# B C of a chunk on eight places of 32 rows by 64 columns in four banks, with the order of work drawn anew

## The chip, the cores and the metric

The kernel runs on one core of one Trainium2 chip. The metric is the device time of one execution in microseconds, the median of several runs. Before the change it is 276.1 us (three runs, 275.99 to 276.71).

## What is computed

A chunked state-space layer feeds a bilinear feed-forward network. `x` is 4 batches x 8 heads x 768 positions x 32; `B` and `C` have a state of 16.

```python
L = np.exp(cum[:, :, :, None] - cum[:, :, None, :]) * causal
CB = np.einsum('bhin,bhjn->bhij', Cc, Bc)
y_intra = np.einsum('bhij,bhjd->bhid', CB * L, xc)
y_inter = np.einsum('bhin,bhnd->bhid', Cc, state) * decay_to_i[:, :, :, None]
state = decay_full[:, :, None, None] * state + np.sum(Bx, axis=2)
...
h = (x @ w1) * (x @ w2) @ w3
return (h @ w_out).astype(np.float32)
```

Here `cum` is the running sum of log `a` within a chunk, and `x` in the last lines is the first part's output, 3072 tokens of 256. The hidden width is 1024. The four weight matrices come as float64.

## The kernel before

**The scan part.** The sequence is cut into 16 chunks of 48 positions. A chunk `c` has 32 sequences (4 batches x 8 heads); two of them share the partitions, so there are 16 groups. Its steps, by name in the written order:

- `B`, `N`, `X` (lines 274 to 276) load B and C for the products (`bc`), B for the state (`bn`) and x (`xe`); `K` loads the running sums.
- `D0`, `D1` (line 300) compute the exponents on TensorE in the first eight chunks; `F` and `G` (lines 321 to 328) do it on VectorE or POOL in the later ones. `E0`, `E1` (line 337) apply Exp into the tile `r`.
- `CB` (line 353) multiplies B with C on TensorE. The operand has 128 rows: two halves `r` of 64 rows, and in each half two groups `p` times the two sequences of a group times the state of 16, with zeros where the rows of one sequence or group meet the columns of another. A product takes 64 rows and 64 columns of the array (rows by `r`, columns by `i`), 96 columns of moving data, and there are 4 x 2 x 2 = 16 of them. The result of half `r` lies in one PSUM bank, so CB takes two banks.
- `M0`, `M1` (line 344, VectorE) multiply `r` by that result; `W0`, `W1` (line 340, POOL) put in the state's part.
- `MX` (line 366) is the product with x and the state, on places of 64 rows by 32 columns.
- `T` (line 382, VectorE) and `Z0` to `Z7` (line 386, on three engines) carry the state into the next chunk's `xe`. `hi`, `lo` (lines 404 to 408) write the output as a rounded part and a rest into `xT`.

**The network part.** A float64 weight is loaded into `st` (`D`), and made into a rounded part and a rest by `A` (ScalarE), `L` and `S` (VectorE), `H` and `P` (any of two engines; line 424 and on). `w0` to `w7` are pieces of w1 and w2, `v00` to `v17` of w3, `o0` to `o3` of w_out. `v..M` (line 491) multiplies w3 by w_out in advance; it gathers in two banks per half for the whole time of that half, and `e` reads them out. The tokens are cut into seven blocks (384, 384, 512 x 4, 256). For block `s` and piece `f`, `ls.f.m` (line 519) has 12 matmuls into two banks, `a` and `g` read them (ScalarE, VectorE), and `h` and `l` split the product. `ds.t.m` (line 563) multiplies by the combined weight, `y` reads the result out and `x` stores it.

**What sets the order.** `PLAN` (line 25) is a list of words, `name:engine` or `name@banks`; each engine executes its words in the order of that list, the loads go to SP's queue in that order (line 137), and the banks of every TensorE step are written into it. `+6@5` stands for six matmuls of zeros that fill TensorE at the start. `st` has four buffers, `mag` five, `fr` four places for the `v` weights, `bc` two.

Of the kernel before, what the change touches and what calls it, by code (L numbers as in the profile page):

```python
# [25 lines left out]
k.act:S k.zero:V k.keep:G t.D +6@5 k.D1:D a.D c0.B c0.N c0.X t.clip:V w0.D t.ln:S k.R0:S c0.Y1:G c1.B +3@7 k.L:S c1.N a.clip:V c0.Y0:G c0.D1@0 a.ln:S  # L26
c1.X w2.D a.scan:V c1.Y1:V +3@7 w1.D a.hi:V c1.Y0:V c0.D0@1 c0.E1:S a.lo:G c0.W1:G c0.CB@2,3 c0.E0:S a.save c0.W0:G c1.D0@4 k.D2:D c0.M1:V c0.M0:V
w0.L:V c0.MX@5,6 w7.D c1.E0:S w0.A:S w0.S:V w0.H:S c1.D1@7 c1.W0:G c0.T:V c0.hi:S w0.P:V c0.Z5:S c0.Z6:S c0.Z1:G c0.lo:V c1.CB@0,1 c0.Z0:S c0.Z4:G
c1.E1:S c0.Z7:V c0.Z2:V c2.B w2.A:S w2.L:V +5@7 c2.N c1.W1:G c1.M0:V c0.Z3:S c1.M1:V w2.S:V c1.MX@2,3 w1.A:S c3.N w1.L:V w6.D c1.hi:S c1.T:V j.m@4
w2.H:V k.R1:S w4.D c1.lo:V +2@7 w2.P:G j.c:S l0.0.m@5,6 w7.A:S c2.K w7.L:V w1.S:V l0.0.a:S w7.S:V c2.CB@7,0 w1.H:V w7.H:S c3.X l0.0.g:V w1.P:G  # L30
l0.2.m@1,2 w3.D w7.P:V l0.2.a:S c2.X w6.L:V w6.A:S l0.1.m@3,4 l0.2.g:V w6.S:V w4.A:S c3.B w4.L:V v11.D w6.H:V l0.1.a:S w5.D w4.S:V c2.D0@5 c2.D1@6
l0.7.m@1,2 c2.E0:S w6.P:G l0.1.g:V c2.E1:S c3.K w4.H:S l0.7.a:S c2.W1:G c4.B w3.A:S w3.L:V l0.6.m@3,5 c2.W0:G c2.M1:V c1.Z4:S o0.D c1.Z3:G c2.M0:V
c1.Z6:G l0.7.g:V c1.Z1:G l0.6.a:S c1.Z0:V c1.Z2:V c5.N c1.Z5:V c1.Z7:V c3.CB@4,6 w3.S:V w4.P:V c2.MX@0,1 w3.H:S l0.6.g:V v11.A:S l0.4.m@7,2 c5.B
c2.T:V c2.hi:S w3.P:V c2.Z0:S c2.Z4:S c2.Z2:G c2.lo:V c2.Z1:S c4.X c2.Z6:S c2.Z5:V w5.A:S w5.L:V v10.D c3.D0@3 c2.Z7:V c3.D1@5 c2.Z3:V c4.N l0.4.a:S
l0.3.m@0,1 v11.L:V c3.E0:S c4.K w5.S:V c3.E1:S c3.W0:G l0.4.g:V w5.H:S c3.W1:G c3.M0:V l0.3.a:S c3.M1:V c4.CB@7,3 w5.P:V o0.A:S a.keep c3.MX@4,5
o0.L:V v11.S:V l0.5.m@2,0 c3.hi:S c3.T:V v11.H:S o0.S:V v11.P:G c3.lo:V l0.5.a:S c3.Z5:S l0.3.g:V o0.H:S l1.7.m@6,2 l0.5.g:V c3.Z2:S c3.Z3:G c3.Z1:S
c3.Z7:V c3.Z4:G c3.Z0:S c5.X v10.A:S v10.L:V o0.P:G c6.B c3.Z6:S l1.7.a:S o1.D c4.D0@4 c4.D1@5 l1.5.m@1,0 c4.E0:S v12.D l1.7.g:V c4.E1:S c5.K c4.W0:G
v10.S:V l1.5.a:S c4.W1:G c4.M0:V v13.D v10.H:V l1.4.m@6,4 v00.D c4.M1:V v10.P:G c7.N l1.5.g:V c6.N l1.4.a:S c4.MX@1,2 l1.4.g:V c5.CB@5,7 o1.A:S o1.L:V
c9.K c4.T:V c4.hi:S l1.6.m@3,0 o1.S:V c4.Z1:S c4.Z5:S c4.Z6:G c4.lo:V c4.Z7:G v12.A:S c4.Z4:V c6.X c4.Z2:G l1.6.a:S c4.Z3:V v01.D c4.Z0:G o1.H:V c7.B
c5.D1@6 c5.D0@4 v12.L:V l1.3.m@1,2 c5.E1:S o1.P:G l1.6.g:V c6.K c5.E0:S v13.A:S l1.3.a:S v12.S:V l1.1.m@3,6 v00.A:S c5.W1:G l1.3.g:V c5.W0:G v12.H:S  # L40
c5.M1:V v03.D v00.L:V l1.1.a:S v12.P:V c6.CB@0,4 c9.F1:G c5.M0:V c8.N l1.1.g:V c8.K c5.MX@1,2 v00.S:V v10.M@7,3 c5.hi:S c9.G1:V v00.H:S c5.T:V c5.lo:V
v01.A:S c5.Z5:G c7.X c5.Z4:G l1.0.m@5,6 c5.Z6:S c5.Z1:V c5.Z3:G c5.Z2:S v00.P:V c5.Z0:S c5.Z7:S c8.B c9.F0:V l1.0.a:S v01.L:V v13.L:V c6.D1@1 c6.D0@2
v01.S:V v11.M@7,3 c6.E1:S c7.K c6.E0:S c6.W1:G l1.0.g:V v03.A:S c6.W0:G c6.M1:V l1.2.m@5,1 c9.N c6.M0:V v01.H:S v13.S:V c8.F0:G l1.2.a:S v02.D v13.H:S
v04.D v12.M@7,3 o3.D v01.P:V c8.G0:G l1.2.g:V c7.D1@2 c7.D0@6 c8.F1:V c6.MX@4,5 c7.E1:S v13.P:G c7.E0:S c7.CB@0,1 c6.T:V c8.X c6.hi:S c6.hj:S c6.lo:V
c8.E0:S c8.CB@2,6 c9.B c6.lp:V c6.Z1:G v02.A:S v02.L:V l2.7.m@4,5 c10.B c6.Z4:G c8.G1:V c7.W1:G c8.E1:S v02.S:V v04.A:S c10.K c6.Z3:G c7.M1:V l2.7.a:S
c8.W0:G v02.H:V l2.0.m@1,4 o3.A:S c7.W0:G c8.M0:V c8.W1:G c10.N c7.M0:V c11.N v02.P:V l2.0.a:S c6.Z5:V c6.Z2:V c6.Z0:V c6.Z6:V v03.L:V c8.M1:V
l2.3.m@2,0 v03.S:V c6.Z7:V v14.D o3.L:V l2.3.a:S c9.G0:V v05.D o3.S:V c10.F1:G l2.0.g:V c7.MX@1,2 o3.H:S l2.3.g:V v13.M@7,3 c7.hi:S c9.X o3.P:G c7.T:V
c9.E0:S c7.lo:V c7.Z7:S c7.Z5:S l2.7.g:V c7.Z0:S c7.Z1:G l2.2.m@6,4 v14.A:S c7.Z4:G v14.L:V c7.Z3:S c9.W0:G c7.Z2:S c9.E1:S v14.S:V l2.2.a:S c11.K
c9.W1:G v05.L:V c12.N c10.G1:G l2.5.m@0,1 l2.2.g:V c7.Z6:V c10.F0:V l2.5.a:S v04.L:V c10.G0:G c8.MX@5,6 l2.5.g:V c11.F1:G v00.M@2,4 c8.hi:S c8.T:V
c10.X c10.E0:S v04.S:V c8.Z4:S c8.Z5:G c8.lo:V c8.Z3:S o2.D c8.Z7:S c11.F0:G l2.6.m@0,1 v15.D c8.Z1:S v03.H:S v17.D c8.Z0:V c10.E1:S c10.W0:G c8.Z6:V  # L50
c12.K l2.6.a:S c10.W1:G c8.Z2:V v03.P:V c13.N v01.M@2,4 c11.G0:V v05.A:S c11.G1:V o2.A:S o2.L:V v05.S:V c9.CB@5,6 o2.S:V v06.D v02.M@2,4 c11.B c9.M0:V
v16.D o2.H:V v14.H:V o2.P:G c9.M1:V l2.4.m@0,5 l2.6.g:V v04.H:V v14.P:G l2.4.a:S v03.M@2,4 v04.P:V v15.L:V v15.A:S v06.L:V v06.A:S v05.H:V v14.M@7,3
v15.S:V v17.A:S v06.S:V v07.D v15.H:S v04.M@2,4 v17.L:V v06.H:V v17.S:V l2.1.m@6,1 v06.P:G l2.4.g:V v16.L:V l2.1.a:S v17.H:V v15.P:V v17.P:G v15.M@7,3
l2.1.g:V v07.L:V c9.MX@5,6 v05.P:V c10.CB@0,1 c12.F1:V v07.A:S c11.X c9.T:V c12.G1:G v16.A:S v05.M@2,4 c10.M0:V c12.B c9.hi:S c10.M1:V c11.E0:S
c9.Z6:G c9.Z4:G c11.E1:S c9.lo:V v16.S:V c9.Z7:S c13.K l3.0.m@0,1 c9.hj:S c11.W0:G v16.H:S c9.lp:V c11.W1:G c9.Z3:V c14.N c9.Z5:V v16.P:V l3.0.a:S
c9.Z0:V c9.Z1:V c12.F0:V v16.M@7,3 c9.Z2:V v07.S:V c12.G0:V v06.M@2,4 v07.H:V c13.F0:V v07.P:G l3.0.g:V v17.M@7,3 c13.F1:V c13.G0:V v07.M@2,4
e11.a:S@3 c13.G1:G e10.a:S@7 e11.b:V@3 e10.b:V@7 l3.4.m@5,6 l0.5.h:S l0.3.h:V l0.4.h:S l0.5.l:V e01.a:S@4 l0.3.l:G l0.7.h:S e01.b:V@4 l1.0.h:S
l0.0.h:V l1.1.h:S l0.7.l:G c10.MX@0,1 e00.a:S@2 c11.CB@3,7 e00.b:V@2 c12.E1:S c12.X l1.1.l:G c12.E0:S c10.T:V l3.7.m@4,2 c10.hi:S c13.B c11.M0:V
l0.4.l:G c10.Z0:S c14.K c11.M1:V c10.Z6:S c10.Z1:S c10.lo:V c10.Z2:G l3.4.a:S l0.1.h:V c12.W0:G l3.4.g:V c12.W1:G l0.1.l:V c15.N l3.1.m@3,7 c10.Z3:G
c10.Z7:V l1.2.h:V l0.0.l:V l0.6.h:V l3.1.a:S l1.0.l:V l0.6.l:G l3.7.a:S l3.6.m@0,1 l3.7.g:V l0.2.h:V c10.Z5:V l0.2.l:G l3.1.g:V l3.6.a:S c10.Z4:V  # L60
c14.F1:V d0.1.m@5 l1.2.l:V c14.G1:G l3.6.g:V c14.F0:V c14.G0:G d0.2.m@6 d0.1.y:S d0.1.x d0.0.m@3 d0.2.y:S d0.2.x l3.2.m@4,2 l1.3.h:S l1.7.h:V l1.4.h:V
l1.6.h:S l1.7.l:V l2.5.h:S l1.3.l:G l3.2.a:S l2.4.h:S l1.6.l:V d0.0.y:S l1.4.l:V c11.MX@0,1 d0.0.x l2.4.l:G l3.2.g:V c12.CB@7,5 c13.E1:S c13.X c11.T:V
c13.E0:S c13.CB@6,4 c11.Z2:S c12.M0:V c14.B c11.Z7:G c11.hi:S c11.Z5:G c15.K c12.M1:V l3.5.m@3,2 c11.Z3:G c11.lo:V c11.Z1:G c13.W1:G c15.B l1.5.h:V
c13.W0:G c13.M1:V l3.5.a:S l1.5.l:G c13.M0:V l2.5.l:V d1.0.m@7 c11.Z6:G l3.5.g:V c11.Z4:G c11.Z0:V c15.F0:V c15.F1:V c15.G0:V d1.1.m@5 c15.G1:V
d1.0.y:S d1.0.x l4.1.m@0,1 d1.1.y:V d1.1.x l4.1.a:S d1.2.m@4 l4.1.g:V l4.5.m@3,6 l2.0.h:S l2.2.h:V l2.3.h:V l2.6.h:S l2.2.l:G d1.2.y:V l2.1.h:S d1.2.x
l2.7.h:S l2.1.l:V l4.4.m@2,7 l2.7.l:G l2.6.l:V l4.4.a:S l2.0.l:G l4.2.m@5,0 l4.4.g:V l2.3.l:G l4.5.a:S l4.5.g:V l4.2.a:S d2.0.m@1 l4.2.g:V d2.1.m@4
d2.0.y:S d2.0.x d2.3.m@2 d2.1.y:V d2.1.x d2.2.m@7 d2.3.y:S d2.3.x l4.6.m@3,6 l3.5.h:S l3.2.h:V l3.7.h:V l3.6.h:S l3.5.l:G l3.1.h:S l4.6.a:S l3.1.l:V
d2.2.y:S d2.2.x l4.7.m@5,0 l3.6.l:G l4.6.g:V l3.7.l:V l4.7.a:S l3.2.l:V l3.0.h:V l4.0.m@1,4 l3.4.h:V l3.0.l:G l4.7.g:V l4.0.a:S l3.4.l:V l3.3.m@2,3
l4.0.g:V l3.3.a:S l4.3.m@7,6 l3.3.g:V l3.3.h:V l3.3.l:G l4.3.a:S c12.MX@0,1 l4.3.g:V d3.0.m@5 c14.E0:S c12.T:V c14.X c12.hi:S c12.Z5:V c12.Z4:G
# [603 lines left out]
```

## Time and profile before

| | before |
|---|---|
| median of three runs | 276.1 us |
| profiled execution | 276.36 us |
| its span on the core | 274.6 us |
| granted TensorE clock | 1.00 |
| TensorE, VectorE, ScalarE, POOL busy | 266.5, 171.6, 112.3, 103.0 us |
| matmuls of CB (64 rows by 64 columns) | 512, 13.6 us busy |
| matmuls of MX (64 rows by 32 columns) | 1024, 14.0 us busy |
| moved by DMA | 36.05 MB |

The span is the time from the first to the last record; the execution's own time lies around it. Times of instructions are their lengths in the record; a matmul's length holds the way through the array, so that matmuls overlap, and how long a burst holds the queue is read from the start of one group to the start of the next. A product of float32 operands shows as two instructions.

### The profile page before, as it was taken

What the parts mean: (1) busy time and instruction counts of PE and PEld (TensorE: products, weight loads), DVE (VectorE), ACT (ScalarE), POOL (GpSimd) and SP (SyncE); (2) the same over time, 40 slices, a digit from 0 to 9 for tenths busy, and PEclk for the clock granted to TensorE, in tenths of its full rate; (3) what the DMA queues carried; (4) which work ended last, traced back from release to release, by engine and by line L of the source; (5) the groups of instructions that cost most, each with busy time, mean ns of one, the idle gap of its engine ahead of it and who ended that gap; (6) DMA issues with size and microseconds to landing.
All of it is one profiled execution on the core that took longest, in us unless ns stands there. A gap on an engine that the chain in (4) does not pass through costs nothing.

```text
span 274.6 us, 7379 instructions
## 1 busy us (share of the span) xinstructions
PE 266.5 (97%) x3019; PEld 236.2 (86%) x3021; DVE 171.6 (62%) x339; ACT 112.3 (41%) x242; POOL 103.0 (38%) x139
## 2 busy tenths in 40 slices
...
GB/s 190 351 339 277 351 191 352 283 291 145 359 232 116 293 245 94 161 0 184 19 21 235 57 21 0 57 22 0 61 58 42 2 33 46 0 0 23 39 19 41
DMA packets 21755, 36.05 MB, mean 131 GB/s; under 512 B 3672, under 2 KB 13528, under 8 KB 21720
## 3 DMA queue, kind: packets, MB, share of 16 engines
...
q8 instruction: 24, 0.39, 0.6%
...
## 4 chain that ended last, share of the span: by engine, by line
PE 87%; DMA 5%; DVE 3%; ACT 2%; issue 1%; DVEq 0%
PE ps L135 87%; DMA st<-in_w3t_dram 4%; DVE mag L450 1%; DMA st<-in_w_out_dram 1%; ACT xT L147 1%; DVE st L144 1%; ACT mag L150 1%; ACT xe L147 0%; DVE xT L141 0%; DVE gs L141 0%; DVE fr L141 0%; ACT wh L147 0%; DVE z L382 0%; ACT gs L147 0%; DVE ob L147 0%
## 5 line engine op out<-in xcount | busy, mean ns | idle before, releaser
L135 PE MATMUL ps<-xT,wh 128*128 128x512 f32 (+2 forms) x448 | 124.7, 362 | 0.7 <-DVE xT L141 0.7
L135 PEld LDWEIGHTS ps<-xT,wh 128*128 128x128 f32 x448 | 79.9, 189 | 11.2 <-DVE xT L141 0.6
L135 PE MATMUL ps<-xT,wl 128*128 128x512 f32 (+2 forms) x224 | 80.4, 359 | 0.0
L135 PE MATMUL ps<-wo,fr 128*128 128x256 f32 x576 | 69.7, 281 | 0.0
L135 PEld LDWEIGHTS ps<-wo,fr 128*128 128x128 f32 x576 | 68.7, 189 | 0.7
L141 POOL TENSOR_TENSOR fr<-gs,fr 128x512 fp32r<-128x512 f32 (+2 forms) x30 | 38.0, 1284 | 78.9 <-PE ps L135 29.0
L147 ACT COPY gs<-ps 128x512 f32<-128x512 f32 (+2 forms) x56 | 29.4, 524 | 65.5 <-PE ps L135 63.8
L141 DVE TENSOR_TENSOR gs<-gs,ps 128x512 f32<-128x512 f32 (+2 forms) x56 | 33.8, 607 | 33.8 <-PE ps L135 25.5
L135 PEld LDWEIGHTS ps<-xT,wl 128*128 128x128 f32 x224 | 42.2, 188 | 5.1
L147 DVE CAST fr<-gs 128x512 fp32r<-128x512 f32 (+2 forms) x29 | 13.4, 470 | 25.3 <-PE ps L135 24.7
L135 PE MATMUL ps<-fr 128*128 128x256 f32 x192 | 25.5, 285 | 0.6 <-DVE fr L141 0.6
L135 PEld LDWEIGHTS ps<-fr 128*128 128x128 f32 x192 | 24.1, 190 | 1.6 <-DVE fr L141 0.8
L141 POOL TENSOR_TENSOR fr<-mag,fr 128x512 fp32r<-128x512 f32 x11 | 15.9, 1447 | 17.8 <-DVE fr L147 14.7
L147 ACT COPY ob<-ps 128x256 f32<-128x256 f32 x16 | 6.0, 373 | 40.0 <-PE ps L135 34.7
L147 POOL COPY xe<-z 16x128 f32<-16x128 f32 x42 | 14.0, 332 | 22.2 <-DVE z L382 12.3
L150 ACT ACTIVATE mag<-st 128x512 f32<-128x512 f32 x28 | 18.5, 673 | 6.9 <-DVE fr L141 5.0
L141 POOL TENSOR_TENSOR r<-bn,r 128x128 f32<-128x128 f32 x32 | 15.9, 511 | 12.7 <-ACT r L150 7.2
L450 DVE SCALAR_TENSOR_TENSOR mag<-mag,st 128x512 uint32<-128x512 uint32 x28 | 19.9, 718 | 1.0 <-ACT mag L150 0.8
L141 DVE TENSOR_TENSOR fr<-gs,fr 128x512 fp32r<-128x512 f32 (+2 forms) x26 | 19.5, 766 | 1.1 <-ACT fr L147 0.9
L141 DVE TENSOR_TENSOR r<-ps,r 128x384 f32<-128x384 f32 x32 | 16.6, 550 | 4.2 <-PE ps L135 3.2
L147 ACT CAST fr<-gs 128x512 fp32r<-128x512 f32 (+2 forms) x27 | 13.8, 560 | 10.5 <-PE ps L135 8.0
L144 DVE TENSOR_SCALAR st<-st 128x512 uint32<-128x512 uint32 x28 | 15.0, 538 | 1.9 <-DMA st<-in_w3t_dram 1.5
...
## 6 DMA issues: line engine op xcount, KB each, us to landing
...
bc<-in_Ct_dram SPq DMA_DIRECT2D x14, 448.0 KB, 7.6
...
```

The source lines that it names most:

```text
L135: pin(nc.tensor.matmul(*args, **kw))
L141: pin((nc.gpsimd if e == "G" else nc.vector).tensor_tensor(*args))
L144: pin(nc.vector.tensor_scalar(*args))
L147: pin(nc.scalar.copy(*args) if e == "S" else (nc.gpsimd if e == "G" else nc.vector).tensor_copy(*args))
L150: pin(nc.scalar.activation(*args, **kw))
L450: pin(nc.vector.scalar_tensor_tensor(d, m, 3, v["wl"].bitcast(U32), ALU.logical_shift_left, ALU.bitwise_or))
```

## The change

Two things change. First, CB: the operand's 128 rows are now four blocks of 32 (`r`, `k`), each with two groups times the state of 16; the two sequences of a group stand beside each other along the free dimension (`i`) and no longer below each other with zeros. The zeros between the two groups stay. The array that the host lays out has 640 instead of 896 numbers a partition. A product takes 32 rows and 64 columns of the array, and there are still 16 of them with 96 columns each. Every block of 32 rows writes a bank of its own, so CB takes four banks, and M reads from two of them. (The code has a form with two banks as well; the order names four banks for all 16 chunks.)

Second, the list `PLAN` is new as a whole: order, engines and banks. Of it: the eight zero matmuls, c0's and c1's four decay steps stand ahead of c0's MX; c2's CB, D0 and D1 stand ahead of the first up step l0.0; the `v` products from v01 to v17 stand between c6's MX and l2.3, with c7 late among them; of the `l` rests 19 (30 before) are on POOL and 37 (26) on VectorE, of the `v` rests 4 (7) on POOL and 12 (9) on VectorE; of the `Z` copies 36 (42) on POOL, 52 (38) on ScalarE and 32 (40) on VectorE.

```diff
-    BC = [sb([P, 4, P + 2 * T], F32, f"bc{i}") for i in range(2)]
+    BC = [sb([P, 2, 2, TE + 2 * T], F32, f"bc{i}") for i in range(2)]
...
         def weigh(hf):
-            gs = slice(hf * HG, (hf + 1) * HG)
-            tt("V", R[:, gs, N:], v["pc", hf], R[:, gs, N:], ALU.mult)
+            w = R[:, hf * HG:(hf + 1) * HG, N:].rearrange("p (k g) s -> p k g s", k=2)
+            tt("V", w, v["pc", hf], w, ALU.mult)
...
         @step("CB")
         def _(e, b):
+            wide = len(b) == 4
             for r in range(2):
-                v["pc", r] = half(b[r]).rearrange("p (g s) -> p g s", s=T)
-            for k in range(4):
-                for r in range(2):
-                    rows = slice(64 * r, 64 * r + 64)
-                    for i in range(2):
-                        cols = slice(64 * i, 64 * i + 64)
-                        mm(psum[b[r]][cols, 2 * T * k:2 * T * (k + 1)], bq[rows, k, cols], bq[rows, k, P:],
-                           start=True, stop=True)
+                if wide:
+                    lo, hi = sorted(b[2 * r:2 * r + 2])
+                    v["pc", r] = PS[:, lo:hi + 1:hi - lo, :4 * T].rearrange("p k (g s) -> p k g s", s=T)
+                else:
+                    v["pc", r] = psum[b[r]][:, :HG * T].rearrange("p (k g s) -> p k g s", k=2, s=T)
+
+            def product(r, k, n, i):
+                rows, cols = slice(64 * r + 32 * k, 64 * r + 32 * k + 32), slice(64 * i, 64 * i + 64)
+                po = v["pc", r][cols, k, 2 * n:2 * n + 2, :].rearrange("p g s -> p (g s)")
+                mm(po, bq[rows, i, n, :TE], bq[rows, i, n, TE:], start=True, stop=True)
+
+            for k in range(2) if not wide else [None]:
+                for n in range(2):
+                    for r in range(2):
+                        for kk in range(2) if wide else [k]:
+                            for i in range(2):
+                                product(r, kk, n, i)
...
-    bq = np.zeros((nch, 2, 2, 2, N, 4, 2 * TE + 2 * T), B.dtype)
+    bq = np.zeros((nch, 4, 2, N, 2, 2, TE + 2 * T), B.dtype)
```

From the new list, the start:

```
k.act:S k.zero:V k.keep:G a.D +8@7 c0.B t.D k.D1:D c0.X k.D2:D a.clip:V a.ln:S w2.D a.scan:V c0.N a.hi:V c0.CB@0,1,2,3 a.lo:V c1.B t.clip:V +3@7
t.ln:S a.save k.R0:V k.L:S c1.N c0.Y0:G w0.D j.m@4 k.R1:S c1.Y1:V c1.X c0.D0@5 c0.Y1:G w2.A:S w2.L:V w3.D c0.D1@6 c1.Y0:G c0.E0:S c2.B w2.S:V c1.D0@7
c0.E1:S c2.N c0.W0:G j.c:V w2.H:S c0.W1:G c0.M0:V c2.K c1.D1@5 w2.P:G c1.E0:S c0.M1:V c0.MX@0,1 c1.W0:G c1.E1:S w0.A:S w0.L:V w5.D c1.CB@6,4,7,2
c1.W1:G c0.T:V +8@5 c0.hi:S w0.S:V c0.Z7:S c0.Z4:S c0.Z0:G c1.M1:V c0.Z6:S c0.Z5:G c0.Z2:S c1.M0:V c0.Z3:S c0.Z1:V w0.H:V c1.MX@2,3 w3.A:S c2.X
c0.lo:V c3.N w0.P:V c1.hi:S c2.CB@5,7,4,6 w6.D c1.T:V c1.lo:V c2.D0@0 w4.D w3.L:V c2.D1@1 l0.0.m@2,3 c2.E0:S w3.S:V c3.K c2.E1:S c2.W0:G w3.H:V
```

More of the change, by code (lines that the diff above doesn't have):

```diff
@@ L25 @@
 PLAN = """
[L26 to L69, printed above, removed]
@@ L70 @@
-c12.Z1:S c12.lo:V c12.Z0:G c14.E1:S c12.Z3:G c12.Z2:V c12.Z6:G c12.Z7:V c14.W0:G c14.W1:G c13.MX@2,3 d3.0.y:S d3.0.x c14.CB@4,7 c13.hi:S c13.T:V c15.X
-c15.E1:S c13.Z1:V c13.Z4:G c13.lo:V c15.CB@6,0 c13.Z2:S c13.Z0:G c13.Z3:S c14.M0:V c13.Z6:G d3.1.m@1 c15.E0:S c15.W1:G c14.M1:V c15.W0:G c15.M1:V
-c13.Z5:V c13.Z7:V c15.M0:V d3.2.m@5 d3.1.y:S d3.1.x c14.MX@2,3 d3.2.y:V d3.2.x d3.3.m@4 c14.hi:S c14.T:V c14.hj:S c14.lo:V c14.Z6:G c14.Z0:S c14.Z1:V
-c14.Z7:G c14.lp:V c14.Z4:V c14.Z3:G c14.Z5:V c14.Z2:G l5.7.m@7,0 l4.7.h:S l4.0.h:V l4.2.h:V l4.1.h:S l4.0.l:G d3.3.y:V l4.4.h:S d3.3.x l4.5.h:S
@@ L74 @@
-l4.3.h:V l4.6.h:S l4.5.l:G c15.MX@5,6 l5.7.a:S l5.0.m@1,2 l5.7.g:V c15.hi:S l4.4.l:G c15.lo:V l4.6.l:V l5.0.a:S l4.1.l:G l6.6.m@3,4 l5.0.g:V l4.2.l:G
-l6.6.a:S l5.3.m@7,0 l6.6.g:V l4.3.l:G l5.3.a:S l4.7.l:V d4.1.m@5 l5.3.g:V d4.3.m@6 d4.1.y:S d4.1.x d4.0.m@1 d4.3.y:S d4.3.x d4.2.m@2 d4.0.y:S d4.0.x
-l5.6.m@3,4 l5.0.h:S l5.3.h:V l5.7.h:V d4.2.y:S l5.3.l:G d4.2.x l5.6.a:S l5.7.l:V l5.5.m@7,0 l5.0.l:G l5.6.g:V l5.6.h:V l5.5.a:S l5.6.l:V l5.4.m@5,6
-l5.5.g:V l5.5.h:V l5.5.l:G l5.4.a:S l5.1.m@1,2 l5.4.g:V l5.4.h:S l5.4.l:G l5.1.a:S l5.2.m@3,4 l5.1.g:V l5.1.h:V l5.1.l:G l5.2.a:S l6.2.m@7,0 l5.2.g:V
@@ new lines @@
+l0.0.a:S c2.W1:G c2.M0:V w5.A:S w3.P:G c2.M1:V l0.2.m@0,1 c5.N c1.Z0:S l0.0.g:V c1.Z2:S c3.B c1.Z5:S c1.Z3:S c1.Z6:V c1.Z7:S w5.L:V c1.Z4:S w5.S:V
+c1.Z1:S l0.2.a:S l0.3.m@2,5 w6.L:V c3.X w6.A:S w5.H:V w7.D l0.2.g:V w5.P:G l0.3.a:S w4.A:S w1.D c2.MX@6,7 l0.3.g:V w4.L:V c3.D1@4 c4.B c2.hi:S w6.S:V
+c3.D0@3 c4.X l0.5.m@0,1 c3.E1:S w4.S:V c4.K w6.H:S c3.W1:G c2.lo:V c3.E0:S w4.H:S w6.P:V l0.5.a:S c3.W0:G c2.T:V c3.CB@2,5,4,3 w4.P:V c2.Z0:S
+l0.6.m@6,7 c2.Z4:S c2.Z3:G c3.M1:V w7.A:S v00.D c2.Z7:G c3.M0:V o0.D c2.Z5:G c2.Z6:G l0.5.g:V l0.6.a:S c2.Z2:V w7.L:V w1.A:S l0.4.m@0,3 c6.N w1.L:V
@@ new lines @@
+c5.E1:S c5.CB@1,7,0,3 c4.hi:S c4.T:V c5.W0:G l1.4.m@2,4 c4.lo:V c5.W1:G c6.X c5.M0:V v01.A:S c7.B c5.M1:V v01.L:V l1.4.a:S o1.S:V c9.K l1.0.m@5,6
+v01.S:V o1.H:S l1.4.g:V l1.0.a:S o1.P:V v11.A:S v11.L:V l1.3.m@1,7 v01.H:V v11.S:V l1.3.a:S v01.P:V v13.D v11.H:S v02.L:V l1.5.m@0,3 c4.Z6:S v12.D
+c4.Z1:G l1.0.g:V c4.Z3:S c4.Z4:G o2.D l1.3.g:V c4.Z5:S v11.P:G v02.A:S c7.N c8.K l1.5.a:S c4.Z7:V c6.D1@2 c4.Z0:V l1.7.m@4,5 c4.Z2:V c6.E1:S c8.N
+v02.S:V c6.W1:G l1.5.g:V l1.7.a:S c9.F0:V v04.D c9.F1:V c5.MX@6,7 c9.G0:G l1.7.g:V c6.CB@1,0,2,3 c5.hi:S c5.T:V c7.X l1.2.m@4,5 v13.A:S c5.Z7:V c8.B
@@ new lines @@
+c5.Z2:G c5.lo:V c5.Z3:G c5.Z6:S c6.M1:V c5.Z4:S c9.G1:G c5.Z5:S c5.Z0:S v12.A:S v12.L:V c6.D0@6 v13.L:V c5.Z1:S v00.M@7,2,-1,-1 l1.2.a:S c7.K v12.S:V
+c6.E0:S v13.S:V o2.A:S v10.M@3,4,-1,-1 c6.W0:G l1.2.g:V v02.H:S c6.M0:V v02.P:V v03.D c6.MX@5,6 c8.F0:V v05.D v12.H:V v01.M@7,2,-1,-1 c9.N c6.hi:S
+o2.L:V c6.hj:S v12.P:V c6.lo:V v04.A:S c8.X o2.S:V l2.6.m@0,1 v13.H:V o3.D o2.H:V v13.P:V l2.6.a:S o2.P:V v04.L:V v02.M@7,2,-1,-1 c8.G0:V v04.S:V
+c8.E0:S v03.A:S c8.W0:G c6.T:V v06.D v11.M@3,4,-1,-1 l2.6.g:V c6.Z4:G c6.Z2:S c6.Z1:S c6.Z7:G c6.lp:V c6.Z3:G v03.L:V v05.A:S l2.0.m@0,1 v05.L:V
@@ new lines @@
+v03.S:V v05.S:V v03.H:S v07.D v04.H:V l2.0.a:S v14.D v03.P:V v04.P:V v03.M@7,2,-1,-1 o3.A:S o3.L:V c6.Z5:V o3.S:V v12.M@3,4,-1,-1 c8.F1:V v17.D
+v06.A:S v06.L:V o3.H:V v06.S:V v04.M@7,2,-1,-1 v05.H:S o3.P:V v16.D v07.A:S v07.L:V v13.M@3,4,-1,-1 v05.P:V v07.S:V v14.A:S v14.L:V v15.D
+v05.M@7,2,-1,-1 c8.G1:V v06.H:S v14.S:V v07.H:S c8.E1:S v06.P:V c7.D1@5 l2.1.m@6,0 v14.H:S c10.K c8.W1:G l2.0.g:V c7.E1:S v14.P:G v17.A:S c11.N
+v16.A:S v07.P:V l2.1.a:S c7.W1:G v06.M@7,2,-1,-1 l2.1.g:V v15.A:S v16.L:V v15.L:V v14.M@3,4,-1,-1 c6.Z6:V v15.S:V c10.F1:G v15.H:S v07.M@7,2,-1,-1
```

52 lines of the change are left out of this document (41 added, 11 removed).

## Prediction

> **What bounds the kernel now.** I read the page first, then the chain of waits, then the busy time by stretch, and last the timeline of TensorE alone.
>
> ```profile
> PE 266.5 (97%) x3019; PEld 236.2 (86%) x3021; DVE 171.6 (62%) x339; ACT 112.3 (41%) x242; POOL 103.0 (38%) x139
> PE 87%; DMA 5%; DVE 3%; ACT 2%; issue 1%; DVEq 0%
> ```
>
> TensorE is busy 97% of 274.6 us and carries 87% of the chain. The chain in order of time says where:
>
> ```profile
> 18.84 38.02 PE ps L135 x494
> ...
> 106.08 164.85 PE ps L135 x1593
> ...
> 270.95 0.42 DVE ob L147
> ```
>
> From 18.84 us to 270.93 us the end hangs on TensorE, with small breaks between 57 and 106 us. Whatever leaves TensorE's queue in that stretch brings the end nearer by as much, as long as no other engine is late. Which engine would be late first, the busy time from 20 to 100 us says (PE, PEld, DVE, ACT, POOL, granted clock, DMA share, GB/s):
>
> ```profile
> 20.00:100.00 80.00, 79.34 (x1088) 72.21 (x1087) 70.11 (x140) 48.31 (x106) 37.75 (x55) 1.00 0.83 267
> ```
>
> VectorE's 140 instructions take 70.1 of these 80 us, 88%; ScalarE and POOL have far more room. So this is a TensorE kernel with VectorE close behind until about 100 us. The granted clock is 1.00 and plays no part.
>
> **The change, part by part.** First the burst of one CB step. On TensorE's timeline (start, length, instructions):
>
> ```profile
> 47.55 0.86 PE L135 MATMUL ps<-r,xe 64*32 64x64 f32 x64
> 48.34 0.89 PE L135 MATMUL ps<-bc 64*64 64x96 f32 x32
> 49.16 0.62 PE L135 MATMUL ps<-xT,wh 128*128 128x384 f32 x2
> ```
>
> A CB step takes 49.16 - 48.34 = 0.82 us of the queue. It has 16 products, and each appears as two instructions. The same burst, cut off after 8 and after 20 of them:
>
> ```profile
> 48.34 0.40 PE L135 MATMUL ps<-bc 64*64 64x96 f32 x8
> ...
> 48.34 0.64 PE L135 MATMUL ps<-bc 64*64 64x96 f32 x20
> ```
>
> Twelve more cost 0.24 us, which is 0.08 us for every four. There are four places (two halves of the rows, two of the columns), so four run side by side and a place is taken for 0.08 us. The MX burst (64x32, eight places) cut off after 16 and after 24:
>
> ```profile
> 47.55 0.34 PE L135 MATMUL ps<-r,xe 64*32 64x64 f32 x16
> ...
> 47.55 0.40 PE L135 MATMUL ps<-r,xe 64*32 64x64 f32 x24
> ```
>
> Eight more cost 0.06 us: eight places do run side by side, and instructions follow each other at 7 ns. The new CB step still has 32 instructions of 96 columns, since the zeros that go lie in the rows: each place has 32 rows in place of 64. They sit on eight places, so four rounds of 0.08 us replace eight, and the last round holds eight places at 7 ns, not four. Of the eight rounds four go (0.32 us) and 0.03 us come back: 0.82 becomes about 0.52, a gain of 0.30 us a step. No row shows places of 32 rows, nor four banks written at once, so I bound it: with no more side by side than now the gain is 0 (the 64x64 row); with the rounds as short as MX's it is 0.35; a loss I exclude, as rows, columns and count per place are at most those of now. I take 0.30, by MX's rows, which have eight places too.
>
> The Trainium skill, TensorE: Matmul & The Clock Gate, in the part on the 56 ns gap, says that start-to-start never falls below about 25 ns, however few columns a matmul has. By that, 32 instructions could not take less than 0.80 us and the gain would be nil. The rows above speak against it here: 64 instructions of MX lie within 0.79 us start to start, 12 ns each.
>
> What of the 16 gains lies on the path? Steps c0 and c1 lie before the dense stretch and c2's is moved ahead of it, which leaves 13 x 0.30 = 3.9 us. The new order puts c2's CB (0.82 today) and its two decay matmuls into the wait for the first xT. They go from the dense stretch whole. A decay matmul is one of 384 columns:
>
> ```profile
> 39.80 0.51 PE L135 MATMUL ps<-xT,wh 128*128 128x384 f32 x2
> 40.15 0.33 PE L135 MATMUL ps<-xT,wl 128*128 128x384 f32 x1
> 40.32 0.51 PE L135 MATMUL ps<-xT,wh 128*128 128x384 f32 x2
> ...
> 68.12 1.55 PE L135 MATMUL ps<-bc 64*64 64x96 f32 x64
> ```
>
> Three in 0.52 us, so 0.17 each: 0.82 + 0.35 = 1.17. The last row takes something back: two CB steps in a row cost 1.55, 0.66 for the second and not 0.82. The order of before has three such pairs (c7 with c8, c12 with c13, c14 with c15), the new one none: 3 x 0.16 = 0.5. Sum for the dense stretch: -3.9 - 1.2 + 0.5 = -4.6 us.
>
> **The start.** Rows of the first 19 us:
>
> ```profile
> 3.06 0.43 SPq L138 DMA_DIRECT2D xe<-in_x_dram  x1
> ...
> 10.52 0.86 PE L135 MATMUL ps<-r,xe 64*32 64x64 f32 x64
> ...
> 15.88 1.13 PE L135 MATMUL ps<-r,xe 64*32 64x64 f32 x64
> ...
> 18.84 0.44 PE L135 MATMUL ps<-xT,wh 128*128 128x384 f32 x1 [0.29 <-DVE xT L141]
> ```
>
> From c0's MX to c1's MX go 5.36 us. Weight w0 is split inside that chain, with both of its ScalarE pieces in front of xT. The new order splits w2 ahead of c0's MX and leaves one ScalarE piece of w0 between. Against that it puts all four decay steps ahead of c0's MX, which I expect about 0.9 us later. I estimate c1's MX 1.5 us earlier and the first up matmul at 17.2 us in place of 18.7. What holds it there is the new second condition: c2's decay matmuls now stand ahead of l0.0 in TensorE's queue, and they wait for c2.K, three loads from the stored sums:
>
> ```profile
> ld<-cq SPq DMA_DIRECT2D x6, 12.0 KB, 4.9
> ```
>
> On SP's queue c2.K now stands behind a.save, w0, c1.X, w3, c2.B and c2.N. At 0.43 us an issue, as in the first row, and with its wait for a.save to land, I put it at 11.5 us, and 4.9 us after that is 16.4, for the last of the three about 17. From 3 us earlier to 1 us later: that is the range of this term; I take -1.5 us.
>
> **VectorE.** The new order gives POOL less (of the low parts of `l` 19 instead of 30, of the P steps of the `v` weights 4 instead of 7) and VectorE more. And the `v` products lie close together: all but v17 come before c7's MX. From c1.lo to c7.M1 the new order has 143 instructions on VectorE: 26 L, 26 S and 17 P of weights, 12 M, 16 products `g` of 384, and 46 smaller ones between the prices of the last two rows.
>
> ```profile
> L144 DVE TENSOR_SCALAR st<-st 128x512 uint32<-128x512 uint32 x28 | 15.0, 538 | 1.9 <-DMA st<-in_w3t_dram 1.5 <-DMA st<-in_w_out_dram 0.2
> L450 DVE SCALAR_TENSOR_TENSOR mag<-mag,st 128x512 uint32<-128x512 uint32 x28 | 19.9, 718 | 1.0 <-ACT mag L150 0.8
> L141 DVE TENSOR_TENSOR fr<-mag,fr 128x512 fp32r<-128x512 f32 x9 | 8.1, 894 | 0.1
> L141 DVE TENSOR_TENSOR r<-ps,r 128x384 f32<-128x384 f32 x32 | 16.6, 550 | 4.2 <-PE ps L135 3.2 <-POOL r L141 0.8
> L141 DVE TENSOR_TENSOR gs<-gs,ps 128x384 f32<-128x384 f32 x16 | 8.7, 547 | 3.5 <-ACT gs L147 1.4 <-ACT mag L150 1.3 <-PE ps L135 0.8
> L141 DVE TENSOR_TENSOR ct<-ct,la 128x384 f32<-128x384 f32 x11 | 7.7, 705 | 3.2 <-DMA ct<-cd 3.2
> L147 DVE COPY xe<-z 16x128 f32<-16x128 f32 x40 | 10.0, 250 | 0.8
> ```
>
> That is 26 x 0.538 + 26 x 0.718 + 17 x 0.894 + 12 x 0.550 + 16 x 0.547 = 63.3 us, and 46 at 0.47 (the middle of 0.25 and 0.705), 21.6: together 84.9. Neighbours overlap, and a step's price hangs on POOL:
>
> ```profile
> 9.44 1.02 DVE L141 TENSOR_TENSOR r<-ps,r 128x384 f32<-128x384 f32 x2 [2.61 <-PE ps L135]
> 10.38 0.43 DVE L144 TENSOR_SCALAR st<-st 128x512 uint32<-128x512 uint32 x1
> ...
> 54.86 0.83 POOL L141 TENSOR_TENSOR ct<-ct,la 128x384 f32<-128x384 f32 x1 [0.93 <-DMA ct<-cd]
> 55.01 0.97 DVE L144 TENSOR_SCALAR st<-st 128x512 uint32<-128x512 uint32 x1
> 55.90 0.68 DVE L141 TENSOR_TENSOR fr<-mag,fr 128x512 fp32r<-128x512 f32 x1
> ```
>
> Two M steps of 0.55 take 1.02, so 0.08 each lies under the neighbour: 84.9 - 143 x 0.08 = 73.5 us. The same L step takes 0.43 with POOL at rest and 0.97 beside it. At the prices of the rest rows (L 0.43, P 0.68) the sum falls by 26 x 0.11 + 17 x 0.21 = 6.4, to 67.
>
> TensorE, from l0.0 to c7's MX, has 16 up steps of 384 and 4 of 512, 15 `v` products, 5 MX, 5 CB and 10 decay matmuls. The rows for the two sizes that are still missing:
>
> ```profile
> 103.70 0.62 PE L135 MATMUL ps<-xT,wh 128*128 128x512 f32 x2
> 104.16 0.39 PE L135 MATMUL ps<-xT,wl 128*128 128x512 f32 x1
> 104.38 0.62 PE L135 MATMUL ps<-xT,wh 128*128 128x512 f32 x2
> ...
> 65.45 1.59 PE L135 MATMUL ps<-fr 128*128 128x256 f32 x12
> 66.88 0.34 PE L135 MATMUL ps<-rd,ld 96*128 96x384 f32 x1
> ```
>
> Three of 512 take 0.68, twelve of a `v` product 1.43. So 16 x 12 x 0.173 + 4 x 12 x 0.227 + 15 x 1.43 + 5 x 0.79 + 5 x 0.52 + 10 x 0.17 = 74 us. VectorE needs 67 to 73.5 of these 74 us, 91 to 99%, where it now has 88%. Any wait of its own for ScalarE or a load then reaches TensorE. Nothing to 6 us; I take +1.5, because POOL is at rest more often in that stage and the low prices are the nearer ones.
>
> **Covered edits.** A CB step's result now lies in four banks until both M steps have read it. The closest successor is c5's CB, which takes banks 0 and 3 about 1.1 us after l1.6 has filled them; the read of 0.547 us covers it if VectorE isn't late, and if it is, that is the term above. M reads two half banks in one instruction of the same 384 elements: I take the same 0.55. The loads of `bc` shrink from 448 to 320 KB each:
>
> ```profile
> bc<-in_Ct_dram SPq DMA_DIRECT2D x14, 448.0 KB, 7.6
> ```
>
> That relieves queues which are 83% busy from 20 to 100 us; no TensorE wait hangs on `bc` now, so I book nothing. The tail after the last matmul has the same steps as before.
>
> **Sum.** -4.6 (dense) - 1.5 (start) + 1.5 (VectorE) = -4.6 us. The profiled execution took 276.36 us (span 274.6 and 1.8 around it), so 271.8 in its terms. It lies 0.26 us over the median of 276.1; so I forecast 271.5.
>
> **The rivals.**
>
> *VectorE takes over in the stage of the `v` products* (slower). For: its 73.5 us at average prices, and the 12% of idle time that it has in the row from 20 to 100 us. 73.5 / 0.88 = 83.5 us is 9.5 more than TensorE's 74, against the 6.1 won elsewhere: 276.1 - 6.1 + 9.5 = 279.5. It decides from the point where that stage lasts over 80 us. Against: part of that idle time is waiting for TensorE, which would vanish, and POOL's lighter load. Chance 0.16.
>
> *The burst does not get shorter*: a floor per instruction, or places of 32 rows that take turns, leaves 0.82. The 3.9 us go; what is left is -1.2 + 0.5 - 1.5 + 1.5 = -0.7, 275.4, which is no change within the 0.3% (0.8 us) that a measurement of this kernel can tell. For: no row has 32 rows. Against: MX's eight places. The page on TensorE cited above would have this result by its floor, and the traces so far leave it little. Chance 0.10.
>
> *Everything falls well*: VectorE at the low prices costs nothing, the start gains 3 us: -4.6 - 3 = -7.6, 268.5. Chance 0.16.
>
> The forecast, with its terms between, has the remaining 0.58. Faster by over 0.3%: 0.58 + 0.16 and a small share of the second rival, 0.76. Within: 0.08. Slower: 0.16. The range goes from 267.0, just below the best case, to 277.5, which takes in the second rival and the first where it decides only just; beyond lie some 0.05 below and 0.14 above.
>
> **What would show it.** In the profile of the changed kernel: CB groups 32x64 with 32 instructions in about 0.5 us start to start, 12 more of them costing about 0.12 us or less where it was 0.24; the first up matmul at about 17 us; TensorE's busy time falling by about 5 us; VectorE over 90% busy from 20 to 90 us. I am wrong on the mechanism if the burst stays near 0.8, on the start if l0.0 begins after 19 us, and on the sum if TensorE shows waits of more than 4 us in total for VectorE between 50 and 95 us: then the new order, not the eight places, sets the time.

## The result, and the profile after

The changed kernel takes 287.4 us (median of four runs, 286.34 to 287.91) against 276.1 for the kernel before (four runs, 275.99 to 276.71): 1.040 times as long, interval 1.037 to 1.043. It is slower, and outside the range of the prediction. The profiled execution took 286.34 us, its span 284.2. Of one kernel below, the one with crosswise pairs, two of four executions ran at a lower mean clock (0.97 and 0.84); its ratio leaves them out, and its rows come from the one at 0.84, so that their times are longer.

Engines and chain of the page after:

```profile
PE 269.3 (95%) x3021; PEld 235.5 (83%) x3021; DVE 171.2 (60%) x347; ACT 115.9 (41%) x253; POOL 82.1 (29%) x120
...
PE 89%; DVE 3%; issue 3%; DMA 2%; ACT 2%; DVEq 0%
```

VectorE does the same amount of work as before (171.2 us against 171.6), and the span is 9.6 us longer. So the bound did not move to another engine's work; something waits. To find where, take the stretch from the first up step to the last matmul: before from 18.84 to 270.71 us, after from 19.97 to 280.24. (Before, one matmul of that step had run alone at 18.03, and the others went on at 18.84. The last matmul's record ends at 270.91 before and 280.59 after, so the stretches stop 0.20 and 0.35 us short of it; differences of the two are good to about 0.2 us.) The two answers of the busy time by stretch (us, then PE, PEld, DVE, ACT, POOL, clock, DMA share, GB/s), before first:

```profile
18.84:270.71 251.87, 250.58 (x2795) 228.60 (x2795) 160.61 (x314) 101.37 (x221) 96.75 (x124) 1.00 0.38 120
```

```profile
19.97:280.24 260.27, 252.14 (x2761) 227.57 (x2762) 159.97 (x323) 104.59 (x230) 74.39 (x104) 0.99 0.35 109
```

Of the 9.5 us by which the second stretch ends later, 1.1 are lost ahead of the first up step and 8.4 behind it. TensorE stands idle for 260.27 - 252.14 = 8.1 us in that stretch, where it was 1.3. The list of waits names one group that grew out of all proportion, the M steps (VectorE, `r` from `ps`; columns are the sum, how often, the longest). After, and behind it the same row of before:

```profile
DVE r L142 <- PE ps L136: 18.9, 11, 3.0
```

```profile
DVE r L141 <- PE ps L135: 3.2, 3, 2.6
```

M waits 18.9 us for TensorE, and the chain in order of time has M pieces on it, which the chain before did not have; four of them:

```profile
102.86 0.57 DVE r L142
...
118.92 0.57 DVE r L142
...
130.80 0.57 DVE r L142
...
195.62 0.02 DVEq L142
195.64 0.04 issue
195.69 0.56 DVE r L142
```

Their length is the 0.55 us that it was. What M waits for, the timeline of TensorE and VectorE shows at c13, whose CB writes the banks 0, 7 (for M0) and 4, 1 (for M1):

```profile
192.05 0.59 PE L136 MATMUL ps<-bc 32*64 32x96 f32 x32
192.57 0.74 PE L136 MATMUL ps<-xT,wh 128*128 128x512 f32 x2
192.92 0.56 DVE L142 TENSOR_TENSOR r<-ps,r 128x384 f32<-128x384 f32 x1
...
195.19 0.39 PE L136 MATMUL ps<-xT,wl 128*128 128x512 f32 x1
195.69 0.56 DVE L142 TENSOR_TENSOR r<-ps,r 128x384 f32<-128x384 f32 x1 [2.21 <-PE ps L136]
...
196.88 1.09 PE L136 MATMUL ps<-r,xe 64*32 64x64 f32 x64 [1.31 <-DVE xe L148]
```

CB is out at 192.64. M1 reads it at 192.92. M0, whose operands are ready by then too, starts at 195.69, right after l4.2.m has ended (195.19 + 0.39 = 195.58). That up step has nothing to do with c13; it writes the banks 5 and 6. Those lie between 0 and 7, the banks of M0, and not between 1 and 4, the banks of M1. On VectorE c12's `lo` and two `Z` copies are queued behind M0, c13's MX waits for the copies, and TensorE stands for 1.31 us.

The late M steps of after follow that pattern (ends and starts are single records; "late" counts from the time when CB was out and VectorE free):

| M | its banks | step that writes between them | its end | M starts | late |
|---|---|---|---|---|---|
| c8.M0 | 2, 5 | v17.M, banks 3, 4 | 102.82 | 102.86 | 1.4 |
| c9.M0 | 2, 5 | d0.1.m, bank 3 | 118.88 | 118.92 | 1.6 |
| c11.M1 | 0, 7 | l3.7.m, banks 1, 5 | 130.77 | 130.80 | 2.0 |
| c13.M0 | 0, 7 | l4.2.m, banks 5, 6 | 195.58 | 195.69 | 2.2 |
| c14.M0 | 4, 7 | l4.6.m, banks 5, 6 | 201.43 | 201.54 | 3.0 |
| c15.M0 | 4, 7 | d3.3.m, bank 5 | 207.29 | 207.40 | 2.9 |

c1.M1, c4.M1, c5.M0 and c12.M1 do the same, for 0.8 to 1.6 us each. All M steps on two neighbouring banks are on time, within 0.3 us, and so are those on banks farther apart when nothing ahead of them in the list writes in between (c13.M1 above, on 1 and 4). So an M waits for every TensorE step that is ahead of it in the list and writes a bank anywhere from its lower to its upper one.

It also holds the other way round. A TensorE step that comes behind such an M in the list and writes a bank between its two waits for M to end. Here l1.0.m on banks 5 and 6 waits for c5.M0 on 1 and 7, and l3.1.m on 2 and 3 for c11.M1 on 0 and 7:

```profile
52.64 0.61 PE L136 MATMUL ps<-xT,wh 128*128 128x384 f32 x2 [0.72 <-DVE r L142]
...
131.42 0.74 PE L136 MATMUL ps<-xT,wh 128*128 128x512 f32 x2 [0.65 <-DVE r L142]
```

The wait is one that the program contains. The piece `DVEq` ahead of M0 in the chain above is an instruction of VectorE's queue that waits for a semaphore; TensorE raises that semaphore at 195.59, when l4.2.m has ended. In the trace all ten late M steps have a wait for TensorE's semaphore, in the instruction itself or in one just ahead of it. The source sets no waits; they come in when the kernel is compiled.

Besides, the granted clock falls to one half for two stretches of 3.4 us, both behind places where TensorE stood idle in the 3.4 us ahead:

```profile
20.00:23.40 3.40, 3.40 (x11) 3.40 (x12) 2.39 (x5) 1.33 (x4) 2.54 (x3) 0.50 0.96 289
122.40:125.80 3.40, 3.40 (x18) 3.40 (x18) 1.76 (x6) 1.29 (x5) 2.93 (x8) 0.50 0.69 202
```

By the granted clock each does 1.7 us of work in 3.4, so I estimate that the two cost 3.4 us. The 24 matmuls that run across the second one take 4.63 us, where 24 of the same shape just ahead take 3.00. That idle time sets off the fall is not shown: in the same execution TensorE stands for 1.31 us up to 196.88 and for 1.40 us up to 208.70, and the clock stays at 1.00.

### The profile page after: what moved, and what is told of

It is laid out like the page before. It is cut to its first block, busy times and chain, and to the rows that moved or that the text cites. A ratio compares the mean times of both kernels' runs of the same rounds, so it can differ in the third digit from the quotient of the medians.

```text
span 284.2 us, 7379 instructions
## 1 busy us (share of the span) xinstructions
PE 269.3 (95%) x3021; PEld 235.5 (83%) x3021; DVE 171.2 (60%) x347; ACT 115.9 (41%) x253; POOL 82.1 (29%) x120
## 4 chain that ended last, share of the span: by engine, by line
PE 89%; DVE 3%; issue 3%; DMA 2%; ACT 2%; DVEq 0%
PE ps L136 89%; DMA bc<-in_Ct_dram 2%; DVE r L142 1%; DVE mag L460 1%; DVE xT L142 1%; ACT mag L151 0%; ACT xe L148 0%; ACT ob L148 0%; DVE xe L148 0%; ACT fr L148 0%; DVE fr L142 0%; DVE gs L142 0%; DVE z L392 0%; ACT xT L148 0%; ACT r L151 0%
## 5 line engine op out<-in xcount | busy, mean ns | idle before, releaser
L136 PE MATMUL ps<-xT,wh 128*128 128x512 f32 (+2 forms) x448 | 126.1, 366 | 2.6 <-DVE r L142 2.0
L136 PE MATMUL ps<-wo,fr 128*128 128x256 f32 x576 | 71.7, 285 | 0.0
L136 PEld LDWEIGHTS ps<-wo,fr 128*128 128x128 f32 x576 | 70.5, 193 | 0.8
L142 POOL TENSOR_TENSOR fr<-gs,fr 128x512 fp32r<-128x512 f32 (+2 forms) x19 | 23.8, 1263 | 89.5 <-DVE fr L148 40.7
L142 DVE TENSOR_TENSOR r<-ps,r 128x384 f32<-128x384 f32 x32 | 16.8, 552 | 19.2 <-PE ps L136 18.9
L142 DVE TENSOR_TENSOR fr<-gs,fr 128x512 fp32r<-128x512 f32 (+2 forms) x37 | 25.7, 720 | 0.8 <-ACT fr L148 0.5
L136 PE MATMUL ps<-fr 128*128 128x256 f32 x192 | 24.6, 284 | 0.0
L136 PEld LDWEIGHTS ps<-r,xe 64*32 64x32 f32 x1024 | 11.9, 105 | 10.5 <-issue 5.0
L136 PE MATMUL ps<-r,xe 64*32 64x64 f32 x1024 | 15.2, 224 | 5.6 <-issue 2.6
L148 POOL COPY xe<-z 16x128 f32<-16x128 f32 x36 | 11.4, 317 | 27.8 <-DVE z L392 18.3
L460 DVE SCALAR_TENSOR_TENSOR mag<-mag,st 128x512 uint32<-128x512 uint32 x28 | 18.9, 685 | 0.6 <-ACT mag L151 0.3
```

Of the source, the lines that this page charges most:

```text
L136: pin(nc.tensor.matmul(*args, **kw))
L142: pin((nc.gpsimd if e == "G" else nc.vector).tensor_tensor(*args))
L148: pin(nc.scalar.copy(*args) if e == "S" else (nc.gpsimd if e == "G" else nc.vector).tensor_copy(*args))
L460: pin(nc.vector.scalar_tensor_tensor(d, m, 3, v["wl"].bitcast(U32), ALU.logical_shift_left, ALU.bitwise_or))
```

## The experiments

My theory: M, one instruction on two banks, is held by steps that write banks between them (span of banks). First rival: the new order as such is late, whatever M reads. Second rival: M's strided read of two banks, or the eight places, is slow in itself, or the memory holds the read up while other banks are written.

**M in two instructions, one for each bank**

```diff
-            w = R[:, hf * HG:(hf + 1) * HG, N:].rearrange("p (k g) s -> p k g s", k=2)
-            tt("V", w, v["pc", hf], w, ALU.mult)
+            for k in range(2):
+                w = R[:, hf * HG + 4 * k:hf * HG + 4 * k + 4, N:]
+                tt("V", w, v["pc", hf][:, k], w, ALU.mult)
```

> Changed kernel, its order and banks untouched, but each M step is two instructions of 192 elements, one for each of its two banks, so that no instruction reads across foreign banks. Theory A (M, one strided read over two banks, is made to wait for every TensorE write to the banks that lie between them): the late starts of M (18.7 us in sum) go, and with them about 11 us of TensorE waits and the two stretches at half clock (3.4 us); 32 more VectorE instructions cost 1 to 3 us of VectorE time. 272 to 277 us. Theory B (the new order itself, with VectorE too full in the stage of the v products and four banks held by CB, costs the time): VectorE only gets more to do, 285 to 290 us.

Measured: 274.7 us (ten runs, 272.94 to 276.06) against 276.5 for before on that chip; ratio 0.994 (0.991 to 0.997). Order, banks and loads are those of the changed kernel. The M group of the changed kernel, and of this one with its 64 instructions (busy time, mean ns, idle time before and its releaser):

```profile
L142 DVE TENSOR_TENSOR r<-ps,r 128x384 f32<-128x384 f32 x32 | 16.8, 552 | 19.2 <-PE ps L136 18.9 <-POOL r L142 0.3
```

```profile
L142 DVE TENSOR_TENSOR r<-ps,r 128x192 f32<-128x192 f32 x64 | 18.4, 345 | 0.5 <-POOL r L142 0.3
```

The wait for TensorE is gone from its row (0.5 us of idle time in all), though the 64 pieces take 18.4 us of VectorE's time where the 32 took 16.8. The first rival falls: the order is not late of itself.

**Same single M, banks drawn anew so that each half has neighbours**

```diff
-c0.CB@0,1,2,3 ... c8.CB@2,5,6,7 ... c13.CB@0,7,4,1 ... c14.CB@4,7,2,3
+c0.CB@0,1,3,4 ... c8.CB@1,2,5,6 ... c13.CB@0,1,4,5 ... c14.CB@4,5,6,7
```

Only bank numbers differ, for all of TensorE's steps; words, engines and their order stay.

> Changed kernel with the same order, engines and instructions; only bank numbers differ: both banks of each half of CB are neighbours, so M reads across nothing foreign and stays one instruction. Theory A: 270 to 276 us, as e1 without its extra instructions, if the new bank numbers bring no waits of their own. Theory B: 285 to 290 us.

Measured: 273.4 us (four runs, 272.7 to 274.43); ratio to before 0.989 (0.985 to 0.994). The same place as above, c13, on this kernel's timeline, and its stretch from the first up matmul to the last:

```profile
183.71 0.59 PE L136 MATMUL ps<-bc 32*64 32x96 f32 x32
...
184.57 1.02 DVE L142 TENSOR_TENSOR r<-ps,r 128x384 f32<-128x384 f32 x2
...
187.17 0.86 PE L136 MATMUL ps<-r,xe 64*32 64x64 f32 x64
```

```profile
19.42:266.95 247.53, 246.67 (x2761) 224.10 (x2762) 159.84 (x323) 104.24 (x230) 74.83 (x104) 1.00 0.36 114
```

Both M steps run back to back as soon as CB is out, MX has no wait in front, and the clock stays at 1.00. In this trace c13's M0 has no wait for a semaphore of TensorE. Between the two kernels, which execute the same words, the stretch differs by 260.27 - 247.53 = 12.7 us: TensorE's idle time by 8.13 - 0.86 = 7.3, the two half-clock stretches by 3.4, and 2.0 that are longer busy time elsewhere and that I have not traced further.

**The new order with the old CB**

The array, the products (64 rows, two banks) and M are those of before; CB takes the first and the third of its four banks.

> The new order with the CB of before: places of 64 rows, two banks (the first and third of the new order's four), the larger bc array. M reads one bank. Theory A: no late M either; CB takes 0.82 us instead of 0.52, 13 times on the path, so 4 us over e2: 275 to 281 us. Theory B: as slow as the changed kernel or slower, 286 to 292 us.

Measured: 277.6 us (ten runs, 276.89 to 280.34); ratio 1.006 (1.004 to 1.009). Its M waits and one CB step:

```profile
DVE r L142 <- PE ps L136: 1.4, 4, 0.6
```

```profile
98.82 0.89 PE L136 MATMUL ps<-bc 64*64 64x96 f32 x32
99.64 1.58 PE L136 MATMUL ps<-fr 128*128 128x256 f32 x11
```

An M in one bank has no late start in the new order. The CB burst holds the queue for 0.82 us as before. Against the kernel with neighbouring banks this is 277.6 - 273.4 = 4.2 us more, and 274.7 - 270.9 = 3.8 by the spans, of which 0.6 lie ahead of the first up step (19.98 against 19.42). The 13 bursts from c3 on differ by 0.30 us each, 3.9 in sum. The two kernels also differ in bank numbers and in the size of the `bc` loads, so about 4 us is what the eight places are worth, and not a clean measure of it. The order alone, with the old CB, wins nothing: 277.6 against 276.5 for before on that chip.

**Neighbouring banks, but paired crosswise from c9 on**

```diff
-c9.CB@0,1,6,7 ... c12.CB@4,5,6,7 ... c13.CB@0,1,4,5 ... c14.CB@4,5,6,7 ... c15.CB@0,1,4,5
+c9.CB@0,6,1,7 ... c12.CB@4,6,5,7 ... c13.CB@0,4,1,5 ... c14.CB@4,6,5,7 ... c15.CB@0,4,1,5
```

The same four banks for each CB; only which two of them M reads together changes.

> As e2_adjacent (order, engines, instructions and the four banks of every CB), but from c9 on the four banks are paired crosswise, first with third and second with fourth, so that M again reads across banks. Between them other TensorE steps write for c9 to c11, c13 and the first half of c15; for c12, c14 and the second half of c15 nothing is written there between CB and M. Theory A: M is late in exactly those, its start following the end of the foreign step by under 0.1 us, and on time in c12, c14 and c15's second M; where MX follows at once (c9, c13, c15) TensorE waits 1 to 2 us each, 276 to 279 us. Rival C (a strided read of two banks that are not neighbours is slow by itself, or banks in use on both sides hold it up in the hardware): M is longer than 0.55 us or late in c12 and c14 as well.

Measured: 283.0, 285.35, 288.72 and 301.76 us; ratio 1.029 (1.023 to 1.035), from the first two. That is slower than the 276 to 279 expected. The rows are of the last. The wait is back:

```profile
DVE r L142 <- PE ps L136: 13.2, 6, 3.5
```

```profile
201.02 0.61 PE L136 MATMUL ps<-bc 32*64 32x96 f32 x32
...
204.41 0.41 PE L136 MATMUL ps<-xT,wl 128*128 128x512 f32 x1
204.85 1.02 DVE L142 TENSOR_TENSOR r<-ps,r 128x384 f32<-128x384 f32 x2 [3.00 <-PE ps L136]
206.52 1.09 PE L136 MATMUL ps<-r,xe 64*32 64x64 f32 x64 [1.70 <-DVE xe L148]
207.53 0.61 PE L136 MATMUL ps<-bc 32*64 32x96 f32 x32
208.27 1.02 DVE L142 TENSOR_TENSOR r<-ps,r 128x384 f32<-128x384 f32 x2
```

At c13 M (banks 0, 4 and 1, 5) waits 3.0 us for l4.2.m on 2 and 3. At c14, in the last two rows, M reads 4, 6 and 5, 7 while l4.6.m again writes 2 and 3, outside: it starts on time, and two M steps take 1.02 us as ever. The same holds at c12. So the second rival falls: reading two banks that are not neighbours costs nothing in itself; a step that writes between them does, through the wait that the program has for it.

The places of the waits came out as expected, the time did not: the expectation counted 1 to 2 us at each of three MX, and the two executions in the ratio lie 9.6 and 12.0 us above 273.4. In the profiled one TensorE's idle times around c9, c10, c13 and c15 are 0.65 to 1.7 us each and 6.7 in sum. What makes up the rest has not been traced.

**Neighbouring banks, and the start in the order of before**

Words up to c1's MX stand as in the kernel before (without its loads of w1, w7 and c3 there), with w0 and not w2 split first; from there on the new order.

> As e2_adjacent, but the words up to c1's MX stand in the order of before (t.D loaded first, c1's two decay steps behind c0's MX; only w1, w7 and c3's loads are left to the new order), bank numbers drawn again with neighbours for CB. It tests the start term of the prediction: the new order's start costs about 0.8 us against that of before, where a gain of 1.5 was forecast. If the four decay steps and the later t.D ahead of c0's MX cost it, c0's MX starts near 10.5 us instead of 12.6 and the first up matmul 1.5 to 2 us earlier than in e2, near 17.7: 271 to 272.5 us. If the chain of weights behind c1's MX holds it, no change: 273 to 274 us.

Measured: 272.65 us (four runs, 272.28 to 272.97); ratio 0.988 (0.984 to 0.991). The median lies 0.7 us below that of the kernel with neighbouring banks, but the two were measured on different chips and their ratios to before overlap (0.984 to 0.991 against 0.985 to 0.994), so the times do not tell them apart. Nor does 272.65 fall into either of the two ranges expected. The traces say more. The start of that one, and of this one:

```profile
12.57 0.86 PE L136 MATMUL ps<-r,xe 64*32 64x64 f32 x64
...
19.42 0.59 PE L136 MATMUL ps<-xT,wh 128*128 128x384 f32 x2 [0.61 <-DVE xT L142]
```

```profile
16.04 0.62 ACT L148 CAST wh<-mag 128x512 fp32r<-128x512 f32 x1 [0.26 <-DVE mag L460]
16.76 0.70 ACT L151 ACTIVATE mag<-st 128x512 f32<-128x512 f32 x1
17.35 0.47 ACT L148 CAST xT<-ps 128x384 fp32r<-128x384 f32 x1
...
18.23 0.52 DVE L142 TENSOR_TENSOR xT<-ps,xT 128x384 fp32r<-128x384 f32 x1
18.89 0.58 PE L136 MATMUL ps<-xT,wh 128*128 128x384 f32 x2 [0.63 <-DVE xT L142]
```

c0's MX starts at 9.70 us here, 2.9 earlier, yet the first up step only 0.5 earlier. What holds it in this kernel is the chain behind c1's MX: two weight pieces on ScalarE (16.04 and 16.76) stand ahead of c1.hi, and the rest `lo` on VectorE ends at 18.75, 0.14 us before the up step.

## Why the prediction was wrong

**The step that failed** stands under the covered edits: "M reads two half banks in one instruction of the same 384 elements: I take the same 0.55." The length was right, 552 ns. What it left out is whom such an instruction waits for. I asked who comes after CB in the same four banks, and not who writes the banks in between. Those waits are most of the 12.7 us by which the two kernels of the same words differ: TensorE's idle time alone is 7.3 of them, more than the whole gain looked for. The two half-clock stretches are 3.4 more, and that they follow from these waits is not shown. That an M waits by span is shown: by the split, by the neighbouring banks and by the crosswise pairs. That it is a wait in the program, and not the memory that holds the read up, the semaphores show. That it is put in because what an access touches is kept as one range from first to last byte is my inference: the source has all eight banks as one tile, and I see in the traces only for whom M waits.

**The signs named in advance** were met in part. The burst is short, so the mechanism of the eight places held. The up steps began after 19 us, so the start term was wrong. But between 50 and 95 us TensorE waits only 0.7 us for VectorE, not over 4: that sign looked for the trouble in the stage of the `v` products, and most of it lies behind it.

**The dense stretch** without that: forecast -4.6, measured 247.53 - 251.87 = -4.3 with neighbouring banks. The burst was forecast at 0.52 us and is 0.52 (101.13 - 100.61 below, after):

```profile
100.61 0.59 PE L136 MATMUL ps<-bc 32*64 32x96 f32 x32
101.13 1.69 PE L136 MATMUL ps<-fr 128*128 128x256 f32 x12
102.86 1.02 DVE L142 TENSOR_TENSOR r<-ps,r 128x384 f32<-128x384 f32 x2 [1.43 <-PE ps L136]
103.47 0.73 PE L136 MATMUL ps<-xT,wh 128*128 128x512 f32 x2 [0.65 <-DVE r L142]
```

The eight places are worth about 4 us by the runs; the 13 steps had been put at 3.9. The rival that the burst does not get shorter falls. 32 instructions start within 0.52 us, 16 ns each; the floor of about 25 ns that the Trainium skill states for back-to-back matmuls in TensorE: Matmul & The Clock Gate, in the part on the 56 ns gap, does not hold here for such small products on places side by side. The two rows below the burst also show the fault itself: M starts at 102.86, after v17 (101.13 + 1.69), and l2.3 waits 0.65 us for M, whose banks it needs.

**The start** was forecast 1.5 us earlier and came 1.1 later (19.97 against 18.84). (The 18.7 of the prediction is 18.84 in its own row, and one up matmul had already run at 18.03.) My sum counted on c1's MX 1.5 us earlier; it comes 1.2 later (17.04 against 15.88). The new order puts all four decay steps of c0 and c1 ahead of c0's MX, where before c1's second stood behind it, and c0's MX starts at 12.3 us where it was 10.5. Part of the rest is the same fault: c1's M1, on banks 2 and 7, waits 1.09 us for the eight matmuls of zeros on bank 5, and with neighbouring banks the first up matmul starts 0.55 us earlier (19.42). Even where c0's MX is early, as in the last experiment, ScalarE's weight pieces ahead of c1.hi decide. c2.K, which I had named as the limit, isn't: c2's decay matmuls run at 18.75, ahead of the last wait.

**VectorE** from 20 to 100 us, after and with neighbouring banks:

```profile
20.00:100.00 80.00, 78.58 (x932) 72.64 (x940) 69.41 (x143) 49.21 (x106) 28.98 (x40) 0.98 0.73 230
```

```profile
20.00:100.00 80.00, 80.00 (x1022) 74.19 (x1021) 71.69 (x149) 52.07 (x113) 31.21 (x45) 1.00 0.75 240
```

VectorE is busy for 71.7 of 80 us, 90%, close to the 91% that I had as its lower bound, and TensorE has no gap at all. The +1.5 was not needed. (The five products in its sum add up to 63.2, not 63.3, which changes nothing.) The slower rival that I had priced, VectorE as the bound, had the sign of the result and not its mechanism: VectorE isn't full when the time is lost, it stands and waits for TensorE, and TensorE then for it.

**The smaller terms.** The loads of `bc` did shrink, land in 3.0 us (7.6 before), and free nothing that TensorE waited for, as booked:

```profile
bc<-in_Ct_dram SPq DMA_DIRECT2D x14, 320.0 KB, 3.0
```

With neighbouring banks the change comes to 273.4 us, 1.9 above the forecast of 271.5. By the spans it is 274.6 - 270.9 = 3.7 us shorter than before, where 4.6 were forecast: the start took 2.1 more than its term (+0.6, not -1.5), the stretch behind it 1.2 less than the -4.6 + 1.5.
